# Decode attention with a gated FFN: K in whole 64 KB rows through a ring of three regions, turned in 8 KB pieces

## The chip, the cores and the metric

The kernel runs on one core of one Trainium2 chip. The metric is the device time of one execution in microseconds. Kernels are compared by the median of several runs.

## The reference

One decode step (one query per sequence, two sequences) of 32-head attention over a cache of 4096 keys is mixed by a gate with a small feed-forward network:

```python
# x [2,1,512]; k_cache, v_cache [2,32,4096,128]; wq [512,4096]; wo [4096,512]; w1 [512,1376]; w2 [1376,512]
g = sigmoid((x * gate_w).sum(-1, keepdims=True))
q = (x @ wq) split into 32 heads of 128
scores = einsum("bhqd,bhkd->bhqk", q, k_cache) * 128 ** -0.5
a = (softmax(scores) applied to v_cache, heads joined) @ wo
b = relu(x @ w1) @ w2
out = g * a + (1 - g) * b
```

All inputs are bf16. K and V hold 64 MB each, wq and wo 4 MB each, w1 and w2 1.4 MB each. Each K and V element is used once.

## The kernel before

**Units.** K and V are read as eight units of 8 MB each. A unit is 32768 rows of 128 values; partition p takes 256 of them in a row, so one unit is 64 KB per partition. Units 0 to 3 belong to the first sequence, 4 to 7 to the second; a unit holds eight heads.

**Order by hand.** Every engine has its own list of instructions, written out by the helpers `sp`, `pe`, `dve`, `act` and `pool`. Waits are named markers (`kt_5` is signalled by turn 5), which become semaphore counts. SP issues all large loads, in the order of its list: wq, w1, K, V, wo, w2, and at the end the store. A load whose wait is not met holds up all that follow in that list.

**K.** `kv` has four slots of 32 KB per partition. K comes in sixteen halves of 4 MB (L239), half n into slot n % 4; a half waits until the second turn of the half four back is done. The fourth slot first holds wq, so half 3 waits for the q projection (`pe_qr1`). VectorE transposes each half in two turns of 128x4096 fp32 elements (two bf16 each, L350, `k_turn`) into one of NKT = 3 buffers of 16 KB in `kt`. For each turn TensorE does 16 matmuls of 512 columns (`k_scores`, L372, and L195 in `held`, which keeps the loaded weights): four weight blocks of q, each used for four PSUM banks. A turn waits for the scores of three turns back. All scores add up in four banks, one row for each piece of keys, so that softmax begins only when the last turn's scores are done.

**q.** `qbuf` holds eight blocks. The first sequence's q is written by four ACT instructions (L315) for all units, the second's by `q_second` (L323) after each of units 0 to 3.

**Softmax.** The maximum over the scores (L378), small steps on VectorE, exponentials on ACT (L393), and transposes back (L397). `spread(u)` writes unit u's probabilities into `ptm` on GpSimd, VectorE and ACT (L407, L409, L411).

**V.** Units 0 to 6 are loaded whole (L242) into two regions of 64 KB, each region two slots of `kv`; unit 7 comes in two halves (L245). V's units 0 and 1 wait for the K turns that free their region, unit u >= 2 waits for `pe_v_{u-2}`, the end of the matmuls of the unit two back (64 matmuls, L423).

**End.** wo goes into slot 0 of `kv` after `pe_v_6` (L247, L248), w2 into `kt` (L249, L251). The projection (L469), the FFN (L479), the sum (L487), a copy (L521) and the store (L252) follow.

Of the kernel before, what the change touches and what calls it, by code (L numbers as in the profile page):

```python
# [85 lines left out]
def bass_gated_mix__gqa_block_cached__dense_activation_relu__decode_kernel(  # L86
# [25 lines left out]
    ez1 = sb("ez1", [128, 2], dt.float32)  # L112
    gb = sb("gb", [128, 2], dt.float32)
    gm = sb("gm", [128, 2], dt.float32)
    kv = sb("kv", [128, 4, 16384], dt.bfloat16)
    kt = sb("kt", [128, NKT, 4096], dt.float32)
    qrow = sb("qrow", [128, 2, 4, 128], dt.bfloat16)
    qbuf = sb("qbuf", [128, 8, 4, 160], dt.bfloat16)
    ptm = sb("ptm", [128, 2, 256, 4, 2], dt.bfloat16)
    mpad = sb("mpad", [128, 32], dt.float32)  # L120
    mrow = sb("mrow", [128, 32], dt.float32)
# [15 lines left out]


    flat = kt[:, :, :].rearrange("p k n -> p (k n)")
    kt16 = flat.bitcast(dt.bfloat16).rearrange("p (k r n two) -> p k r n two", k=NKT, r=128, two=2)  # L140
    w1 = flat[:, 0:2752].bitcast(dt.bfloat16)
    E = flat[:, 0:2048].bitcast(dt.bfloat16)
    ET = flat[:, 2048:4096].bitcast(dt.bfloat16)
    w2 = flat[:, 4096:4096 + 2816].bitcast(dt.bfloat16).rearrange("p (r n) -> p r n", n=512)
    X2 = flat[:, 7168:7168 + 1024].rearrange("p (u d) -> p u d", d=128)
    Y = flat[:, 8192:8192 + 512]
    YW = flat[:, 8704:8704 + 512]

    PSF = nc.alloc_psum_tensor("PS", [128, 4096], dt.float32)
    PSB = PSF[:, :].bitcast(dt.bfloat16)  # L150
# [1 line left out]
    def psf(p0, p1, c0, n):  # L152
        return PSF[p0:p1, c0:c0 + n]
# [17 lines left out]
        P.sems[e] = nc.alloc_semaphore(e + "_ev")  # L171
    names = ["x", "gw", "wq", "w1", "wo0", "wo1", "w2a", "w2b", "w2c", "w2d", "out"]
    sem = {n: nc.alloc_semaphore("sem_" + n) for n in names}
    sem_k = [nc.alloc_semaphore(f"sem_k{s}") for s in range(4)]
    sem_v = [nc.alloc_semaphore(f"sem_v{s}") for s in range(3)]

    mk = {}
# [48 lines left out]
    def unit_in(rows, u):  # L226
        return rows[u * 32768:(u + 1) * 32768, :].rearrange("(p r) d -> p (r d)", p=128)

    region = kv[:, :, :].rearrange("p (g s) n -> p g (s n)", g=2)
    wq_sb = kv[:, 3, :].rearrange("p (t u h e d) -> p t u h e d", t=4, u=4, h=4, e=2)  # L230
    wo_sb = kv[:, 0, :]

    act(lambda e: e.dma_start(x_sb[0:2, :], A_x.rearrange("b s d -> (b s) d")).then_inc(sem["x"], 16))
    act(lambda e: e.dma_start(x_sb[2:3, :], gate_w.rearrange("(o d) -> o d", o=1)).then_inc(sem["gw"], 16))
    sp(lambda e: e.dma_start(kv[:, 3, :], wq_in).then_inc(sem["wq"], 16))
    sp(lambda e: e.dma_start(w1, w1_in).then_inc(sem["w1"], 16))
    for n in range(16):
        u, hf = divmod(n, 2)
        sp(lambda e, n=n, u=u, hf=hf: e.dma_start(kv[:, n % 4, :], unit_in(k_rows, u)[:, 16384 * hf:16384 * (hf + 1)]).then_inc(sem_k[n % 4], 16),  # L239
           waits=([f"kt_{2 * (n - 4) + 1}"] if n >= 4 else ["pe_qr1"] if n == 3 else []))  # L240
    for u in range(7):
        sp(lambda e, u=u: e.dma_start(region[:, u % 2, :], unit_in(v_rows, u)).then_inc(sem_v[u % 2], 16),  # L242
           waits=([f"pe_v_{u - 2}"] if u >= 2 else ["kt_27"] if u == 0 else ["kt_31"]))
    for hf in range(2):
        sp(lambda e, hf=hf: e.dma_start(kv[:, 2 + hf, :], unit_in(v_rows, 7)[:, 16384 * hf:16384 * (hf + 1)]).then_inc(sem_v[1 + hf], 16),  # L245
           waits=(["pe_v_5"] if hf == 0 else []))
    sp(lambda e: e.dma_start(wo_sb[:, 0:12288], wo_in[:, 0:12288]).then_inc(sem["wo0"], 16), waits=["pe_v_6"])  # L247
    sp(lambda e: e.dma_start(wo_sb[:, 12288:16384], wo_in[:, 12288:16384]).then_inc(sem["wo1"], 16))  # L248
    sp(lambda e: e.dma_start(w2[0:96, 10, :], B_w2[1280:1376, :]).then_inc(sem["w2a"], 16))  # L249
    for name, r0, r1 in (("w2b", 0, 5), ("w2c", 5, 9), ("w2d", 9, 10)):  # L250
        sp(lambda e, name=name, r0=r0, r1=r1: e.dma_start(w2[:, r0:r1, :], w2_in[:, r0:r1, :]).then_inc(sem[name], 16))  # L251
    sp(lambda e: e.dma_start(out.rearrange("b s (c n) -> (b s c) n", n=256), out_sb[0:128:32, :]).then_inc(sem["out"], 16),  # L252
# [35 lines left out]
    def q_proj():  # L288
        for n in range(8):
            for t in range(4):  # L290
                pe(lambda e, n=n, t=t: e.matmul(  # L291
                    psf(32 * (n % 4), 32 * (n % 4) + 32, (QR_B + n // 4) * BANK, 512), lhsT=xTw[:, t, :],
                    rhs=wq_sb[:, t, n // 2, :, n % 2, :], start=(t == 0), stop=(t == 3), tile_position=(0, 32 * (n % 4))),
                   dwaits=([(sem["wq"], 16)] if n == 0 and t == 0 else []),
                   waits=(["dve_xTw"] if n == 0 and t == 0 else []),
                   signal=(f"pe_qr{n // 4}" if n % 4 == 3 and t == 3 else None))
        for half in range(2):
            row = psf(0, 128, (QR_B + half) * BANK, 512).rearrange("p (h e d two) -> p e h d two", h=4, e=2, two=2)
            for e2 in range(2):
                dst = qrow[:, half, 2 * e2:2 * e2 + 2, :].rearrange("p two (h d) -> p h d two", h=4)  # L300
                src = row[:, e2]
                if half:
                    act(lambda a, dst=dst, src=src: a.activation(out=dst, in_=src, func=ACT.Copy),
                        waits=[f"pe_qr{half}"], signal=f"qrow{half}{e2}")
                else:
                    dve(lambda v, dst=dst, src=src: v.tensor_copy(out=dst, in_=src), waits=[f"pe_qr{half}"], signal=f"qrow{half}{e2}")
        for half in range(2):
            for j in range(4):
                pe(lambda e, half=half, j=j: e.transpose(qT_ps[:, (4 * half + j) * 128:(4 * half + j + 1) * 128],
                                                         qrow[:, half, j, :], ident16[:, :]),  # L310
                   waits=([f"qrow{half}{e2}" for e2 in range(2)] if j == 0 else []),
                   signal=("pe_q" if half and j == 3 else None))
        cols = qT_ps.rearrange("p (f j s m) -> p f s j m", f=2, j=4, s=4)
        for hq in range(4):
            act(lambda a, hq=hq: a.activation(  # L315
                out=qbuf[32 * hq:32 * hq + 32, :, :, 32 + 32 * hq].rearrange("p (f s) j -> p f s j", f=2),
                in_=cols[32 * hq:32 * hq + 32, :, :, :, 0], func=ACT.Copy),
                waits=["pe_q", "c_qbuf"], signal=f"q_0_{hq}")

    def q_second(u):  # L320
        cols = qT_ps.rearrange("p (f j s m) -> p f s j m", f=2, j=4, s=4)
        for hq in range(4):
            act(lambda a, hq=hq: a.activation(  # L323
                out=qbuf[32 * hq:32 * hq + 32, 2 * u:2 * u + 2, :, 32 + 32 * hq],
                in_=cols[32 * hq:32 * hq + 32, u // 2, 2 * (u % 2):2 * (u % 2) + 2, :, 1], func=ACT.Copy),
                waits=[f"pe_sc_{4 * u + 3}"], signal=f"q_1_{u}_{hq}")

    def ffn_h():
        for ft in range(11):
# [14 lines left out]
                signal=f"dve_h{b}")  # L344

    def k_turn(i):
        n, h = divmod(i, 2)
        pairs = kv[:, n % 4, :].bitcast(dt.float32).rearrange("p (r h d) -> p h r d", h=2, d=32)
        dst = kt[:, i % NKT, :].rearrange("p (r n) -> p r n", n=32)
        dve(lambda v: v.transpose(out=dst, in_=pairs[:, h]),  # L350
            waits=([f"pe_sc_{i - NKT}"] if i >= NKT else ["pe_h"] if i == 0 else []),
            dwaits=([(sem_k[n % 4], 16 * (n // 4 + 1))] if h == 0 else []), signal=f"kt_{i}")

    def k_scores(i):
        n, h = divmod(i, 2)
        u, hf = divmod(n, 2)
        for two in range(2):
            for e2 in range(2):
                pos = 4 * u + 2 * hf + e2
                w = qbuf[:, 2 * (u % 4) + e2, 2 * h + two, 32 - pos:160 - pos]  # L360
                first, last = i == 0 and two == 0 and e2 == 0, i == 31 and two == 1 and e2 == 1
                for bk in range(4):
                    head = two == 0 and e2 == 0 and bk == 0
                    waits = [f"kt_{i}"] if head else []
                    if head and i % 4 == 0:
                        waits += [f"q_{u // 4}_{u % 4}_{hq}" if u >= 4 else f"q_0_{hq}" for hq in range(4)]

                    def fn(e, bk=bk, w=w, e2=e2, two=two, first=first, last=last):
                        args = (psf(0, 128, bk * BANK, 512), w, kt16[:, i % NKT, 32 * bk:32 * bk + 32, 16 * e2:16 * e2 + 16, two])
                        if bk:  # L370
                            return held(e, *args, first, last)
                        return e.matmul(args[0], lhsT=args[1], rhs=args[2], start=first, stop=last)  # L372
                    pe(fn, waits=waits, signal=(f"pe_sc_{i}" if two == 1 and e2 == 1 and bk == 3 else None))
        if i % 4 == 3 and u < 4:
            q_second(u)

    def softmax():
        dve(lambda v: v.tensor_reduce(out=mpad[:, 0:1], in_=psf(0, 128, 0, 2048), axis=AX.X, op=ALU.max),  # L378
            waits=["pe_sc_31", "c_mpad"], signal="dve_m")
        dve(lambda v: v.transpose(out=mrow[:, :], in_=mpad[:, :]), waits=["dve_m"], signal="dve_mt")  # L380
        dve(lambda v: v.tensor_reduce(out=mmax[:], in_=mrow[:, :].rearrange("p (u f e) -> p u e f", f=2, e=2), axis=AX.X, op=ALU.max),
            waits=["dve_mt"], signal="dve_mm")
# [108 lines left out]
    gate()  # L491
    selectors()
    q_proj()
    ffn_h()
    for i in range(32):
        k_turn(i)
        if i >= 1:
            k_scores(i - 1)
    k_scores(31)
    softmax()  # L500
    denominators()
    spread(0)
# [51 lines left out]
```

## Time and profile before

| | us |
|---|---|
| median of 3 runs | 345.94 (345.84 to 347.35) |
| the profiled execution | 346.09 |
| its span, first to last instruction | 344.6 |
| busy: TensorE / VectorE / ScalarE / GpSimd | 190.7 / 176.1 / 18.8 / 21.6 |
| moved by DMA | 145.57 MB, mean 422 GB/s |

The span is one profiled execution. PE is TensorE, PEld its weight loads, DVE VectorE, ACT ScalarE, POOL GpSimd, SP the engine that issues the loads. A line "start us, us, engine, line, operation, tiles xcount [idle before <- releaser]" is a row of the timeline. A row of the stretches gives the window, its length, busy time (and instructions) of PE, PEld, DVE, ACT and POOL, the granted TensorE clock, the DMA share and GB/s. The chain of waits is the chain of work that ended last, followed back from the last instruction.

### The profile page before, as it was taken

How to read it: one execution, taken by the hardware profiler on the slowest of the kernel's cores; microseconds unless marked ns; L12 is line 12 of the kernel's file. 1: busy time of each engine (PE TensorE's matmuls, PEld its weight loads, DVE VectorE, ACT ScalarE, POOL GpSimd, SP SyncE). 2: the span in 40 equal slices, each digit the busy share in tenths (PEclk: the TensorE clock that was granted, in tenths of full speed). 3: DMA queues.
4: the chain of work that ended last, by engine and by line, in shares of the span. 5: the costliest groups of instructions: out<-in, count | busy, mean ns of one | idle time of the engine just before them, and what ended most of it. 6: DMA issues, size and time to landing. Idle time of an engine off the chain costs nothing.

```text
span 344.6 us, 2345 instructions
## 1 busy us (share of the span) xinstructions
PE 190.7 (55%) x1226; PEld 40.6 (12%) x842; DVE 176.1 (51%) x93; ACT 18.8 (5%) x48; POOL 21.6 (6%) x33
## 2 busy tenths in 40 slices
PE   0432988877787779877785053215070603215456
PEld 0230100000000000000000021002030201102122
DVE  0708988888998888888985730202010020201021
ACT  1030000000000000000000700000000000000000
POOL 8300000000000000000000230101010010100000
PEclk9965899999999999999999586858567675856566
DMA  8999999999999999999998999999998999999995
GB/s 320 453 424 426 426 426 434 434 415 437 453 436 426 434 426 426 426 426 432 469 464 388 479 398 449 403 457 443 403 479 388 464 413 434 418 411 443 417 415 186
DMA packets 4743, 145.57 MB, mean 422 GB/s; under 512 B 535, under 2 KB 766, under 8 KB 1022
## 3 DMA queue, kind: packets, MB, share of 16 engines
q1 hardware_dynamic: 4728, 145.43, 98.3%
q8 instruction: 8, 0.13, 0.2%
q10 hardware_dynamic: 6, 0.00, 0.0%
q14 instruction: 1, 0.01, 0.0%
HBM read 145.43 MB, written 0.00 MB: 422 GB/s over the span
## 4 chain that ended last, share of the span: by engine, by line
DMA 76%; DVE 12%; PE 9%; ACT 1%; issue 1%; POOL 0%; SPq 0%; DVEq 0%
DMA kv<-in_A_k_cache_dram 38%; DMA kv<-in_A_v_cache_dram 27%; DVE kt L350 10%; DMA kt<-in_B_w_dram 7%; PE PS L423 6%; DMA kv<-in_A_wq_dram 4%; ACT kt L393 1%; PE PS L291 1%; PE PS L195 1%; DVE mpad L378 1%; PE PS L479 1%; POOL ptm L407 0%; DVE kt L397 0%; PE PS L372 0%; PE PS L487 0%
## 5 line engine op out<-in xcount | busy, mean ns | idle before, releaser
L350 DVE STREAM_TRANSPOSE kt<-kv 128x4096 f32<-128x4096 f32 x32 | 140.3, 4424 | 18.9 <-DMA kv<-in_A_k_cache_dram 18.9
L195 PE MATMUL PS<-kt,qbuf 128*128 128x512 bf16 x384 | 113.0, 403 | 0.0
L423 PE MATMUL PS<-kv,ptm 128*32 128x512 bf16 x512 | 45.8, 534 | 86.0 <-DMA kv<-in_A_v_cache_dram 84.9
L372 PE MATMUL PS<-kt,qbuf 128*128 128x512 bf16 x128 | 52.0, 406 | 35.8 <-DVE kt L350 35.8
L429 DVE TENSOR_TENSOR kt<-PS,maskc 128x512 f32<-128x512 f32 x8 | 5.5, 692 | 117.3 <-PE PS L423 117.3
L423 PEld LDWEIGHTS PS<-kv,ptm 128*32 128x32 bf16 x512 | 18.5, 128 | 112.2 <-issue 100.4
L372 PEld LDWEIGHTS PS<-kt,qbuf 128*128 128x128 bf16 x128 | 12.5, 98 | 150.2 <-issue 77.6
L407 POOL COPY ptm<-kt 32x512 bf16<-32x512 bf16 x16 | 11.1, 696 | 273.8 <-DVE rsum L437 184.6
L411 ACT ACTIVATE ptm<-kt 32x512 bf16<-32x512 bf16 x8 | 5.1, 652 | 95.8 <-PE PS L423 94.5
L393 ACT ACTIVATE kt<-PS,negm 128x512 bf16<-128x512 f32 x8 | 5.4, 696 | 80.2 <-DVE negm L389 80.2
L433 DVE TENSOR_REDUCE kt<-kt 128x128 f32<-128x512 f32 x8 | 8.2, 1028 | 0.3
L323 ACT ACTIVATE qbuf<-PS 32x8 bf16<-32x8 bf16 x16 | 3.1, 196 | 85.1 <-PE PS L195 84.8
L440 PE MATMUL PS<-rsum,sell 128*32 128x1 f32 x4 | 0.4, 197 | 10.1 <-DVE rsum L437 10.1
L397 DVE STREAM_TRANSPOSE kt<-kt 128x1024 bf16<-128x1024 bf16 x4 | 5.0, 1245 | 1.7 <-ACT kt L393 1.4
L258 PE MATMUL PS<-ident,x_sb 3*128 3x3 bf16 x4 | 0.3, 168 | 8.1 <-DMA x_sb<-in_gate_w_dram 8.1
L261 DVE COPY xT<-PS 128x12 bf16<-128x12 bf16 x1 | 0.2, 169 | 8.4 <-PE PS L258 8.4
L205 POOL MEMSET qbuf<- 128x5120 bf16 x1 | 4.4, 4358 | 0.0
L378 DVE TENSOR_REDUCE mpad<-PS 128x1 f32<-128x2048 f32 x1 | 2.3, 2291 | 4.0 <-PE PS L195 4.0
L469 PE MATMUL PS<-kv,oW 128*2 128x512 bf16 x32 | 3.7, 621 | 1.1 <-DMA kv<-in_A_wo_dram 1.1
L291 PE MATMUL PS<-kv,xTw 128*32 128x512 bf16 x32 | 3.6, 631 | 0.5 <-DMA kv<-in_A_wq_dram 0.5
L217 POOL MEMSET ptm<- 128x4096 bf16 x1 | 3.5, 3501 | 0.0
L409 DVE COPY ptm<-kt 32x512 bf16<-32x512 bf16 x8 | 3.1, 383 | 0.2
(62 smaller groups left out, 45.2 us busy)
## 6 DMA issues: line engine op xcount, KB each, us to landing
kv<-in_A_k_cache_dram SPq DMA_DIRECT2D x16, 4096.0 KB, 30.0
kv<-in_A_v_cache_dram SPq DMA_DIRECT2D x2, 4096.0 KB, 28.0
kv<-in_A_wq_dram SPq DMA_DIRECT2D x1, 4096.0 KB, 12.2
kv<-in_A_wo_dram SPq DMA_DIRECT2D x1, 3072.0 KB, 20.4
kt<-in_B_w_dram SPq DMA_DIRECT2D x1, 1376.0 KB, 15.0
kv<-in_A_wo_dram SPq DMA_DIRECT2D x1, 1024.0 KB, 22.8
kt<-in_B_w_dram SPq DMA_DIRECT2D x1, 640.0 KB, 23.7
kt<-in_B_w_dram SPq DMA_DIRECT2D x1, 512.0 KB, 24.5
```

Of the source, the lines that this page charges most:

```text
L195: return e.add_instruction(mybir.InstMatmult(start_tensor_calc=start, stop_tensor_calc=stop, tile_size=(128, 128), tile_position=(0, 0), l ...
L291: pe(lambda e, n=n, t=t: e.matmul(psf(32 * (n % 4), 32 * (n % 4) + 32, (QR_B + n // 4) * BANK, 512), lhsT=xTw[:, t, :], rhs=wq_sb[:, t, n ...
L350: dve(lambda v: v.transpose(out=dst, in_=pairs[:, h]), waits=([f"pe_sc_{i - NKT}"] if i >= NKT else ["pe_h"] if i == 0 else []), dwaits=([ ...
L372: return e.matmul(args[0], lhsT=args[1], rhs=args[2], start=first, stop=last)
L378: dve(lambda v: v.tensor_reduce(out=mpad[:, 0:1], in_=psf(0, 128, 0, 2048), axis=AX.X, op=ALU.max), waits=["pe_sc_31", "c_mpad"], signal=" ...
L393: act(lambda a, bk=bk, e2=e2: a.activation(out=blocks[:, bk, :, 16 * e2:16 * e2 + 16], in_=psf(0, 128, bk * BANK, 512).rearrange("p (r n) ...
L397: dve(lambda v, bk=bk: v.transpose(out=ET[:, 1024 * bk:1024 * bk + 1024], in_=E[:, 1024 * bk:1024 * bk + 1024]), waits=[f"act_exp{bk}{e2}" ...
L407: pool(lambda e, args=args: e.tensor_copy(**args), waits=waits, signal=f"pt_{u}_{hq}")
L411: act(lambda e, args=args: e.activation(func=ACT.Copy, **args), waits=waits, signal=f"pt_{u}_{hq}")
L423: pe(lambda e, m=m, t=t: e.matmul(psf(32 * t, 32 * t + 32, V_B[u % 2] * BANK, 512), lhsT=ptm[:, u % 2, 4 * m:4 * m + 4, :, :], rhs=rows[:, ...
L429: dve(lambda e: e.tensor_tensor(out=Y.rearrange("p (c d) -> p c d", c=4), in0=psf(0, 128, V_B[u % 2] * BANK, 512).rearrange("p (c d) -> p ...
L433: dve(lambda e: e.tensor_reduce(out=X2[:, u, :], in_=Y.rearrange("p (c d) -> p d c", c=4), axis=AX.X, op=ALU.add), waits=[f"dve_y{u}"], si ...
```

## The change

- `kv` gets a fifth slot of 32 KB. K moves in ten segments instead of sixteen halves: units 1 to 6 whole, 8 MB each, into the two 64 KB regions in turn; units 0 and 7 in halves of 4 MB, into the fifth slot. The order is u0 first half, u1, u2, u0 second half, u3, u4, u7 first half, u5, u6, u7 second half. A segment waits for the last turn of the segment three back; segment 2 for the q projection.
- The buffers of `kt` shrink from 16 to 8 KB per partition. A turn transposes 128x2048 elements, so there are 64 of them, each with 8 matmuls on two of the four banks (the other `rr`, the other two banks).
- `qbuf` holds two segments' blocks instead of all eight. `q_put(g)` writes the block of segment g (four ACT instructions) after the scores of segment g - 2.
- wo is loaded into the fifth slot and waits for the last turn (`kt_63`); w2 moves to the start of `kt` and waits for the spread of unit 7. Their place in SP's list, behind V's unit 7, is as before. `ET`, `X2`, `Y` and `YW` move within `kt` and `qbuf`.

```diff
-    kv = sb("kv", [128, 4, 16384], dt.bfloat16)
-    kt = sb("kt", [128, NKT, 4096], dt.float32)
+    kv = sb("kv", [128, 5, 16384], dt.bfloat16)
+    kt = sb("kt", [128, NKT, 2048], dt.float32)
...
-    qbuf = sb("qbuf", [128, 8, 4, 160], dt.bfloat16)
+    qbuf = sb("qbuf", [128, 2, 2, 4, 160], dt.bfloat16)
...
-    wo_sb = kv[:, 0, :]
+    wo_sb = kv[:, 4, :]
+    segments = [(0, (0,)), (1, (0, 1)), (2, (0, 1)), (0, (1,)), (3, (0, 1)), (4, (0, 1)), (7, (0,)), (5, (0, 1)), (6, (0, 1)), (7, (1,))]
+    pieces = []
+    for g, (u, halves) in enumerate(segments):
+        for hf in halves:
+            for h in range(2):
+                for rr in range(2):
+                    pieces.append((g, u, hf, h, rr))
...
+    def place(g):
+        return (4, 0, 2)[g % 3]
...
-    for n in range(16):
-        u, hf = divmod(n, 2)
-        sp(lambda e, n=n, u=u, hf=hf: e.dma_start(kv[:, n % 4, :], unit_in(k_rows, u)[:, 16384 * hf:16384 * (hf + 1)]).then_inc(sem_k[n % 4], 16),
-           waits=([f"kt_{2 * (n - 4) + 1}"] if n >= 4 else ["pe_qr1"] if n == 3 else []))
+    for g, (u, halves) in enumerate(segments):
+        dst = kv[:, 4, :] if len(halves) == 1 else region[:, place(g) // 2, :]
+        src = unit_in(k_rows, u)[:, 16384 * halves[0]:16384 * (halves[-1] + 1)]
+        sp(lambda e, g=g, dst=dst, src=src: e.dma_start(dst, src).then_inc(sem_k[g % 3], 16),
+           waits=([f"kt_{last_of[g - 3]}"] if g >= 3 else ["pe_qr1"] if g == 2 else []))
     for u in range(7):
         sp(lambda e, u=u: e.dma_start(region[:, u % 2, :], unit_in(v_rows, u)).then_inc(sem_v[u % 2], 16),
-           waits=([f"pe_v_{u - 2}"] if u >= 2 else ["kt_27"] if u == 0 else ["kt_31"]))
+           waits=([f"pe_v_{u - 2}"] if u >= 2 else [f"kt_{last_of[7]}"] if u == 0 else [f"kt_{last_of[8]}"]))
...
-    sp(lambda e: e.dma_start(wo_sb[:, 0:12288], wo_in[:, 0:12288]).then_inc(sem["wo0"], 16), waits=["pe_v_6"])
+    sp(lambda e: e.dma_start(wo_sb[:, 0:12288], wo_in[:, 0:12288]).then_inc(sem["wo0"], 16), waits=["kt_63"])
...
-    sp(lambda e: e.dma_start(w2[0:96, 10, :], B_w2[1280:1376, :]).then_inc(sem["w2a"], 16))
+    sp(lambda e: e.dma_start(w2[0:96, 10, :], B_w2[1280:1376, :]).then_inc(sem["w2a"], 16),
+       waits=[f"pt_7_{hq}" for hq in range(4)])
...
+    def q_put(g):
+        b, u4 = divmod(segments[g][0], 4)
         cols = qT_ps.rearrange("p (f j s m) -> p f s j m", f=2, j=4, s=4)
         for hq in range(4):
             act(lambda a, hq=hq: a.activation(
+                out=qbuf[32 * hq:32 * hq + 32, g % 2, :, :, 32 + 32 * hq],
+                in_=cols[32 * hq:32 * hq + 32, u4 // 2, 2 * (u4 % 2):2 * (u4 % 2) + 2, :, b], func=ACT.Copy),
+                waits=(["pe_q", "c_qbuf"] if g < 2 else [f"pe_sc_{last_of[g - 2]}"]), signal=f"q_{g}_{hq}")
...
     def k_turn(i):
-        n, h = divmod(i, 2)
-        pairs = kv[:, n % 4, :].bitcast(dt.float32).rearrange("p (r h d) -> p h r d", h=2, d=32)
+        g, u, hf, h, rr = pieces[i]
+        slot = place(g) + (hf if len(segments[g][1]) == 2 else 0)
+        pairs = kv[:, slot, :].bitcast(dt.float32).rearrange("p (r h d) -> p h r d", h=2, d=32)
         dst = kt[:, i % NKT, :].rearrange("p (r n) -> p r n", n=32)
-        dve(lambda v: v.transpose(out=dst, in_=pairs[:, h]),
+        dve(lambda v: v.transpose(out=dst, in_=pairs[:, h, 64 * rr:64 * rr + 64]),
             waits=([f"pe_sc_{i - NKT}"] if i >= NKT else ["pe_h"] if i == 0 else []),
-            dwaits=([(sem_k[n % 4], 16 * (n // 4 + 1))] if h == 0 else []), signal=f"kt_{i}")
+            dwaits=([(sem_k[g % 3], 16 * (g // 3 + 1))] if i == first_of[g] else []), signal=f"kt_{i}")
...
-                for bk in range(4):
+                for bk in range(2):
...
-                        args = (psf(0, 128, bk * BANK, 512), w, kt16[:, i % NKT, 32 * bk:32 * bk + 32, 16 * e2:16 * e2 + 16, two])
+                        args = (psf(0, 128, (2 * rr + bk) * BANK, 512), w, kt16[:, i % NKT, 32 * bk:32 * bk + 32, 16 * e2:16 * e2 + 16, two])
```

More of the change, by code (lines that the diff above doesn't have):

```diff
@@ L139, in bass_gated_mix__gqa_block_cached__dense_activation_relu__decode_kernel @@
     flat = kt[:, :, :].rearrange("p k n -> p (k n)")
-    kt16 = flat.bitcast(dt.bfloat16).rearrange("p (k r n two) -> p k r n two", k=NKT, r=128, two=2)
+    kt16 = flat.bitcast(dt.bfloat16).rearrange("p (k r n two) -> p k r n two", k=NKT, r=64, two=2)
     w1 = flat[:, 0:2752].bitcast(dt.bfloat16)
     E = flat[:, 0:2048].bitcast(dt.bfloat16)
[L143 to L147, printed above, removed]
+    ET = flat[:, 4096:6144].bitcast(dt.bfloat16)
+    w2 = flat[:, 0:2816].bitcast(dt.bfloat16).rearrange("p (r n) -> p r n", n=512)
+    X2 = flat[:, 3072:4096].rearrange("p (u d) -> p u d", d=128)
+    qflat = qbuf[:, :, :, :, :].rearrange("p s e j c -> p (s e j c)").bitcast(dt.float32)
+    Y = qflat[:, 0:512]
+    YW = qflat[:, 512:1024]
     PSF = nc.alloc_psum_tensor("PS", [128, 4096], dt.float32)
@@ L173, in bass_gated_mix__gqa_block_cached__dense_activation_relu__decode_kernel @@
     sem = {n: nc.alloc_semaphore("sem_" + n) for n in names}
-    sem_k = [nc.alloc_semaphore(f"sem_k{s}") for s in range(4)]
+    sem_k = [nc.alloc_semaphore(f"sem_k{s}") for s in range(3)]
     sem_v = [nc.alloc_semaphore(f"sem_v{s}") for s in range(3)]
@@ L227, in unit_in @@
         return rows[u * 32768:(u + 1) * 32768, :].rearrange("(p r) d -> p (r d)", p=128)
-    region = kv[:, :, :].rearrange("p (g s) n -> p g (s n)", g=2)
+    region = kv[:, 0:4, :].rearrange("p (g s) n -> p g (s n)", g=2)
     wq_sb = kv[:, 3, :].rearrange("p (t u h e d) -> p t u h e d", t=4, u=4, h=4, e=2)
-    wo_sb = kv[:, 0, :]
+    wo_sb = kv[:, 4, :]
[6 more added lines that the diff above has]
+                    pieces.append((g, u, hf, h, rr))
+    last_of = {p[0]: i for i, p in enumerate(pieces)}
+    first_of = {}
+    for i, p in enumerate(pieces):
+        first_of.setdefault(p[0], i)
+    def place(g):
+        return (4, 0, 2)[g % 3]
     act(lambda e: e.dma_start(x_sb[0:2, :], A_x.rearrange("b s d -> (b s) d")).then_inc(sem["x"], 16))
@@ L315, in q_proj @@
             act(lambda a, hq=hq: a.activation(
[L316 to L326, printed above, removed]
+                out=qbuf[32 * hq:32 * hq + 32, g % 2, :, :, 32 + 32 * hq],
+                in_=cols[32 * hq:32 * hq + 32, u4 // 2, 2 * (u4 % 2):2 * (u4 % 2) + 2, :, b], func=ACT.Copy),
+                waits=(["pe_q", "c_qbuf"] if g < 2 else [f"pe_sc_{last_of[g - 2]}"]), signal=f"q_{g}_{hq}")
     def ffn_h():
@@ L346, in k_turn @@
     def k_turn(i):
-        n, h = divmod(i, 2)
-        pairs = kv[:, n % 4, :].bitcast(dt.float32).rearrange("p (r h d) -> p h r d", h=2, d=32)
+        g, u, hf, h, rr = pieces[i]
+        slot = place(g) + (hf if len(segments[g][1]) == 2 else 0)
+        pairs = kv[:, slot, :].bitcast(dt.float32).rearrange("p (r h d) -> p h r d", h=2, d=32)
         dst = kt[:, i % NKT, :].rearrange("p (r n) -> p r n", n=32)
-        dve(lambda v: v.transpose(out=dst, in_=pairs[:, h]),
+        dve(lambda v: v.transpose(out=dst, in_=pairs[:, h, 64 * rr:64 * rr + 64]),
             waits=([f"pe_sc_{i - NKT}"] if i >= NKT else ["pe_h"] if i == 0 else []),
-            dwaits=([(sem_k[n % 4], 16 * (n // 4 + 1))] if h == 0 else []), signal=f"kt_{i}")
+            dwaits=([(sem_k[g % 3], 16 * (g // 3 + 1))] if i == first_of[g] else []), signal=f"kt_{i}")
     def k_scores(i):
-        n, h = divmod(i, 2)
-        u, hf = divmod(n, 2)
+        g, u, hf, h, rr = pieces[i]
         for two in range(2):
@@ L359, in k_scores @@
                 pos = 4 * u + 2 * hf + e2
-                w = qbuf[:, 2 * (u % 4) + e2, 2 * h + two, 32 - pos:160 - pos]
-                first, last = i == 0 and two == 0 and e2 == 0, i == 31 and two == 1 and e2 == 1
-                for bk in range(4):
+                w = qbuf[:, g % 2, e2, 2 * h + two, 32 - pos:160 - pos]
+                first, last = i < 2 and two == 0 and e2 == 0, i > 61 and two == 1 and e2 == 1
+                for bk in range(2):
                     head = two == 0 and e2 == 0 and bk == 0
                     waits = [f"kt_{i}"] if head else []
-                    if head and i % 4 == 0:
-                        waits += [f"q_{u // 4}_{u % 4}_{hq}" if u >= 4 else f"q_0_{hq}" for hq in range(4)]
+                    if head and i == first_of[g]:
+                        waits += [f"q_{g}_{hq}" for hq in range(4)]
                     def fn(e, bk=bk, w=w, e2=e2, two=two, first=first, last=last):
-                        args = (psf(0, 128, bk * BANK, 512), w, kt16[:, i % NKT, 32 * bk:32 * bk + 32, 16 * e2:16 * e2 + 16, two])
+                        args = (psf(0, 128, (2 * rr + bk) * BANK, 512), w, kt16[:, i % NKT, 32 * bk:32 * bk + 32, 16 * e2:16 * e2 + 16, two])
                         if bk:
@@ L372, in fn @@
                         return e.matmul(args[0], lhsT=args[1], rhs=args[2], start=first, stop=last)
-                    pe(fn, waits=waits, signal=(f"pe_sc_{i}" if two == 1 and e2 == 1 and bk == 3 else None))
-        if i % 4 == 3 and u < 4:
-            q_second(u)
+                    pe(fn, waits=waits, signal=(f"pe_sc_{i}" if two == 1 and e2 == 1 and bk == 1 else None))
+        if i == last_of[g] and g + 2 < len(segments):
+            q_put(g + 2)
     def softmax():
         dve(lambda v: v.tensor_reduce(out=mpad[:, 0:1], in_=psf(0, 128, 0, 2048), axis=AX.X, op=ALU.max),
-            waits=["pe_sc_31", "c_mpad"], signal="dve_m")
+            waits=["pe_sc_63", "c_mpad"], signal="dve_m")
         dve(lambda v: v.transpose(out=mrow[:, :], in_=mpad[:, :]), waits=["dve_m"], signal="dve_mt")
@@ L493, in bass_gated_mix__gqa_block_cached__dense_activation_relu__decode_kernel @@
     q_proj()
+    q_put(0)
+    q_put(1)
     ffn_h()
-    for i in range(32):
+    for i in range(64):
         k_turn(i)
@@ L498, in bass_gated_mix__gqa_block_cached__dense_activation_relu__decode_kernel @@
             k_scores(i - 1)
-    k_scores(31)
+    k_scores(63)
     softmax()
```

## The prediction

> **What bounds the kernel now.** I read the page first (engines, slices), then the chain of waits, SP's own waits, and last the timeline of VectorE and TensorE around the seam between K and V.
>
> ```profile
> span 344.6 us, 2345 instructions
> PE 190.7 (55%) x1226; PEld 40.6 (12%) x842; DVE 176.1 (51%) x93; ACT 18.8 (5%) x48; POOL 21.6 (6%) x33
> DMA  8999999999999999999998999999998999999995
> DMA packets 4743, 145.57 MB, mean 422 GB/s; under 512 B 535, under 2 KB 766, under 8 KB 1022
> ```
>
> No compute engine is busy for more than 55%, while the DMA row stands at 9 in nearly every slice. The chain names DMA for 76% of the span. So the time is bytes over rate, plus whatever gaps the queue has. The stretches by windows give the rate in the two long phases:
>
> ```profile
> 60.00:160.00 100.00, 80.43 (x328) 7.94 (x83) 90.48 (x22) 2.35 (x12) 0.00 (x0) 1.00 1.00 430
> 210.00:300.00 90.00, 28.49 (x332) 12.59 (x332) 11.02 (x17) 3.29 (x5) 6.39 (x10) 0.69 0.99 430
> 315.00:339.00 24.00, 11.62 (x108) 4.22 (x112) 4.01 (x6) 0.00 (x0) 0.00 (x0) 0.62 0.99 413
> ```
>
> The last columns are the granted clock, DMA share and GB/s. K (first row, rows of 32 KB) and V (second, rows of 64 KB) move at the same 430. Bytes do not change, so the edit can only win or lose gaps, and a gap needs SP to issue a load later than the load ahead of it ends. SP's waits are long (L239 122.4 us in 12 times): each load is issued long before its turn. The place to watch is the seam:
>
> ```profile
> 163.62 8.77 DVE L350 STREAM_TRANSPOSE kt<-kv 128x4096 f32<-128x4096 f32 x2 [1.03 <-DMA kv<-in_A_k_cache_dram]
> 173.34 8.77 DVE L350 STREAM_TRANSPOSE kt<-kv 128x4096 f32<-128x4096 f32 x2 [0.94 <-DMA kv<-in_A_k_cache_dram]
> 186.14 2.29 DVE L378 TENSOR_REDUCE mpad<-PS 128x1 f32<-128x2048 f32 x1 [4.03 <-PE PS L195]
> ...
> 197.75 5.38 PE L423 MATMUL PS<-kv,ptm 128*32 128x512 bf16 x64 [1.16 <-POOL ptm L407]
> 212.10 5.04 PE L423 MATMUL PS<-kv,ptm 128*32 128x512 bf16 x64 [8.97 <-DMA kv<-in_A_v_cache_dram]
> 231.45 5.59 PE L423 MATMUL PS<-kv,ptm 128*32 128x512 bf16 x64 [14.32 <-DMA kv<-in_A_v_cache_dram]
> ```
>
> K's last 4 MB land at 173.3 and are turned in 8.8 us; softmax and V's unit 0 follow; its end at 203.17 lets SP issue V's unit 2. V's unit 1 lands at 212.0, so that issue has 8.8 us to spare. Landings are 9.72 us apart for 4 MB of K, and 19.35 for 8 MB of V.
>
> **Part 1, whole rows for K's units 1 to 6.** Two K halves take 19.44 us, one V unit 19.35: 0.09 us less for 8 MB in rows of 64 KB. Six units: 0.5 us gained. The bounds are 0 (the windows show 430 for both) and 0.6.
>
> [...]
>
> **Part 2, pieces of 8 KB.** 32 turns become 64. A 128x4096 transpose takes 4.42 us, two take 8.77 (start to start 4.35); a 128x32 one (L389) takes 0.19. The line through both gives 0.19 + 2016 x 1.042 ns = 2.29 us for 2048 elements, 2.22 start to start with the same overlap of 0.07. Bounds: half of 4.35, 2.18, and 2.33 if nothing overlaps. Per 4 MB that is 8.9 us against 8.77, below the 9.72 in which they arrive.
>
> TensorE does 8 matmuls for each piece with four weight loads (128 more in all). In the old pieces matmuls start every 0.236 us, and the group's first, which carries the weight load, comes no later than the others (four in 0.94). So 1.9 us a piece; 2.3 if each of the four loads (98 ns) showed in full. I take 1.9: VectorE stays the slower of the two, or level. With three buffers a turn waits for the scores of three pieces back, 4.4 us old, and never stalls.
>
> The new ACT writes (40 of 0.2 us, in place of 4 and 16) come a whole segment ahead of their reader: 9 us or more cover them, nothing else runs on ACT there, and uncovered one set costs 0.8. The memset of qbuf is halved on GpSimd, beside the first load. Both at 0.
>
> **Part 3, the ring.** In units of 4 MB the segments land at 1, 3, 5, 6, 8, 10, 11, 13, 15 and 16, the last four at 124.7, 144.1, 163.6 and 173.3 us. Each is turned at 8.9 us per 4 MB from its landing or the end of the one before. A load waits for the segment three back. Segment 4, for example, waits for segment 1: landed 46.9, turned 64.7; the load ahead of it ends at 76.0. Segments 5, 7, 8 and V's units 0 and 1 have the same 11 us; the others more. No gap there.
>
> The price comes at the end. Before, only 4 MB were unturned when K's last byte landed. Now segment 8 (8 MB) lands at 163.6 and segment 9 queues behind it: twelve pieces, 163.62 + 11 x 2.22 + 2.29 = 190.3, against 182.1. The scores after the last turn shrink from 4.02 to 2.14 us (eight matmuls fewer, 1.88). From the maximum to the end of V's unit 0 is as before, 203.17 - 186.14 = 17.03 us. So V's unit 2 is issued at 190.3 + 2.14 + 17.03 = 209.5, 6.3 us later than now. Behind it on SP only later V loads wait, which are due later.
>
> Is that too late? The first load shows 12.20 us from issue to landing for 4 MB, 2.48 more than the steady 9.72. Issued at 209.5, unit 2 lands at 209.5 + 2.48 + 19.35 = 231.3: when it lands now. Cost 0. The trace's landing records are harsher: twelve of sixteen DMA engines end unit 1 at 210.1 to 210.4, four at 211.2 to 212.0. First packets come 1.0 us after issue and take 2.0 us where steady ones take 1.21, so the early twelve lose about 209.5 + 1.0 - 210.2 + 0.8 = 1.1 us. That lead is not free: the 16 KB instruction fetches each throw one engine back by 1 to 1.7 us, and by the end nine have been hit, some after this point. Between 0 and 1.1 I take 0.8, nearer the packet records.
>
> **Part 4, wo and w2.** Their issue moves from 315.0 to about 295.5, behind V's last halves in SP's order (w2 also behind the last spread, some 1.5 us). The order in the queue is unchanged, and at 315.0 the queue still held V's data until 328. Cost and gain 0. Y and YW in qbuf and E's places change no duration.
>
> **Sum.** The profiled execution took 346.09 (span 344.6 and 1.5 around it), 0.15 over the median 345.94. 346.09 - 0.5 + 0.8 = 346.4.
>
> **Rivals.**
> 1. Slower: V's unit 2 comes clearly late. From 210.2 on (packet records) or 209.5 (landings) each us of delay is a us of time. A piece of 2.33 adds 1.3; V's unit 0 at the 6.14 us that unit 6 takes adds 0.8; scores of 2.5 after the last turn add 0.4. Together the issue is at 212.0 and the gap 2.5 to 3.6: 348.1 to 349.2. Against it: the transpose is regular and its price leaves little room. It decides against "no change" from an issue at about 210.5.
> 2. TensorE's clock falls in the gaps between segments. The row 17:56 of the stretches shows 0.78 after a long idle; half speed means 1.69 us for four matmuls (32.03 to 33.72), 3.4 for a piece. New gaps are 10 us after segment 0 and 2 to 3 us later. The two pieces in hand absorb most of it; before segment 8 it would push the issue by up to 1 us: about 347.4. Against it: the clock stays at 1.00 from 56 to 182 us with waits of 1.6. By the Trainium skill ("TensorE: Matmul & The Clock Gate", Part 1) the clock falls after an idle window of about 3.4 us, which only the first gap reaches; a fall there has 11 us of slack.
> 3. Faster: the end improves because wo and w2 are queued early. The stretch 315:339 runs at 413 against 431; were all of that the late issue, 24 x 18/431 = 1.0 us comes back, with 0.3 in the 19 us ahead: 346.09 - 0.5 - 1.3 = 344.3. Against it: the share is 0.99 there; the rows are 1 to 24 KB, and stay so.
> 4. Much faster: each K load carries a fixed cost like the first load's 2.48 us, and six loads fewer save 14.9 us: 331. Against it: the spacings of 9.72 and 19.35 leave no room for it.
>
> **How the numbers follow.** My sum 0.58; rival 1 0.27, rival 2 0.07, rival 3 0.07, rival 4 0.01. About 0.5% (1.7 us) is what a measurement of this kernel tells from no change, so the sum and half of rival 2 count as same, rival 1 and the rest of rival 2 as slower, and rivals 3 and 4 mostly as faster. Range: downwards 346.09 - 0.6 less half of rival 3's gain, 345.0; upwards rival 1's end, 349.2.
>
> **What would show it.** The turns at 2.2 us start to start and the last one ending near 190; the reduce of the maximum near 192.5; SP issuing V's unit 2 near 209.5 and V's unit 2 landing near 231.3 to 232; K at 19.35 per 8 MB; PEclk at 1.00 through K after 60 us. I am wrong if V's unit 2 lands past 233, if VectorE waits for TensorE within a segment, or if the stretch after 315 changes its rate.

## The result, and the profile after

The changed kernel takes 347.85 us (median of 22 runs, 345.88 to 349.21), the kernel before 346.78 us beside it. The ratio is 1.003, 95% interval 1.0017 to 1.0043: slower by 1.07 us in the medians, and within the 0.5% that the prediction calls no change. 346.4 had been forecast against 345.94, 0.5 us more; the measured difference is twice that, and inside the range. Single executions of 386 us and more (one of the 22 of the kernel before here) are left out of every ratio.

The page of the changed kernel has the same shape: DMA carries the chain, no engine is the bound.

```profile
span 346.5 us, 2520 instructions
PE 199.0 (57%) x1226; PEld 54.3 (16%) x970; DVE 175.1 (51%) x125; ACT 22.3 (6%) x68; POOL 19.5 (6%) x33
DMA  8998998999999998998999999899998999989993
```

The timeline at the seam between K and V (start us, us, engine, line, operation, tiles, count, idle before and its releaser) is the one to lay beside that of before:

```profile
143.76 17.66 DVE L365 STREAM_TRANSPOSE kt<-kv 128x2048 f32<-128x2048 f32 x8 [2.74 <-DMA kv<-in_A_k_cache_dram]
163.00 26.43 DVE L365 STREAM_TRANSPOSE kt<-kv 128x2048 f32<-128x2048 f32 x12 [1.58 <-DMA kv<-in_A_k_cache_dram]
191.59 2.29 DVE L392 TENSOR_REDUCE mpad<-PS 128x1 f32<-128x2048 f32 x1 [2.15 <-PE PS L196]
...
203.20 5.80 PE L437 MATMUL PS<-kv,ptm 128*32 128x512 bf16 x64 [1.16 <-POOL ptm L421]
211.45 5.09 PE L437 MATMUL PS<-kv,ptm 128*32 128x512 bf16 x64 [2.46 <-DMA kv<-in_A_v_cache_dram]
232.32 4.90 PE L437 MATMUL PS<-kv,ptm 128*32 128x512 bf16 x64 [15.78 <-DMA kv<-in_A_v_cache_dram]
...
209.05 0.33 SPq L260 DMA_DIRECT2D kv<-in_A_v_cache_dram  x1
```

Twelve pieces in one row: segment 8 lands at 163.0 and VectorE turns without a pause until 189.43, through segment 9. The maximum starts at 191.59 (186.14 before). The last row is SP's: V's unit 2 is issued at 209.05, where it was 203.17. V's unit 1 is ready at 211.45, 0.65 us earlier than before (212.10). Unit 2 is ready at 232.32, 20.87 us later, though 8 MB need 19.35: a gap of 1.52 us in the stream of loads, and unit 2 is now 0.87 us late. From there on the loads are evenly spaced again, and the delay stays to the end. The chain of waits shows the end (start us, us, what):

```profile
299.70 41.45 DMA kt<-in_B_w_dram
341.19 1.23 PE PS L493 x10
342.43 0.85 PE PS L501 x4
343.28 1.07 PE PS L493 x11
344.37 0.42 DVE out_sb L537
```

The part of w2 that the chain names lands at 299.70 + 41.45 = 341.15. In the kernel before it was 316.36 + 23.71 = 340.07:

```profile
316.36 23.71 DMA kt<-in_B_w_dram
340.11 1.24 PE PS L479 x20
...
342.40 0.42 DVE out_sb L521
```

So w2 lands 1.08 us later, close to the difference of the medians. The profiled spans differ by more, 1.9 us, because TensorE took 3.2 us behind that landing in place of 2.3. That is the granted clock of this one execution. The stretches show it (PE, PEld, DVE, ACT, POOL busy, then granted clock, DMA share, GB/s), first the changed kernel, then the kernel before:

```profile
337.30:344.20 6.90, 5.64 (x76) 1.88 (x68) 0.69 (x1) 0.00 (x0) 0.00 (x0) 0.51 0.53 198
```

```profile
341.30:344.60 3.30, 1.05 (x32) 0.45 (x20) 0.42 (x1) 0.00 (x0) 0.00 (x0) 1.00 0.00 1
```

The times of the kernel before suggest that it does this too in half of its runs: 21 of its 22 times lie at 345.75 to 346.43 and at 346.76 to 347.47. The experiments take up both: the gap, and the end.

### The profile page after: what moved, and what is told of

The parts are those of the page before. It is cut to its first block, busy times and chain, and to the rows that moved or that the text cites. A ratio compares the mean times of both kernels' runs of the same rounds, so it can differ in the third digit from the quotient of the medians.

```text
span 346.5 us, 2520 instructions
## 1 busy us (share of the span) xinstructions
PE 199.0 (57%) x1226; PEld 54.3 (16%) x970; DVE 175.1 (51%) x125; ACT 22.3 (6%) x68; POOL 19.5 (6%) x33
## 4 chain that ended last, share of the span: by engine, by line
DMA 76%; PE 12%; DVE 11%; issue 0%; SPq 0%; DVEq 0%
DMA kv<-in_A_k_cache_dram 32%; DMA kv<-in_A_v_cache_dram 29%; DMA kt<-in_B_w_dram 12%; DVE kt L365 10%; PE PS L437 5%; DMA kv<-in_A_wq_dram 4%; PE PS L386 3%; PE PS L196 2%; PE PS L310 1%; PE PS L493 1%; DVE kt L447 0%; PE PS L501 0%; DVE qbuf L443 0%; DVE out_sb L537 0%; DVE ptm L423 0%
## 5 line engine op out<-in xcount | busy, mean ns | idle before, releaser
L365 DVE STREAM_TRANSPOSE kt<-kv 128x2048 f32<-128x2048 f32 x64 | 141.2, 2274 | 25.4 <-DMA kv<-in_A_k_cache_dram 25.4
L386 PE MATMUL PS<-kt,qbuf 128*128 128x512 bf16 x256 | 107.2, 419 | 33.8 <-DVE kt L365 29.4
L196 PE MATMUL PS<-kt,qbuf 128*128 128x512 bf16 x256 | 106.8, 417 | 0.0
L443 DVE TENSOR_TENSOR qbuf<-PS,maskc 128x512 f32<-128x512 f32 x8 | 5.5, 692 | 113.2 <-PE PS L437 113.2
L386 PEld LDWEIGHTS PS<-kt,qbuf 128*128 128x128 bf16 x256 | 25.9, 101 | 142.8 <-issue 72.9
L337 ACT ACTIVATE qbuf<-PS 32x8 bf16<-32x8 bf16 x40 | 7.8, 196 | 137.5 <-PE PS L196 136.2
L447 DVE TENSOR_REDUCE kt<-qbuf 128x128 f32<-128x512 f32 x8 | 8.2, 1029 | 0.3
L325 DVE CAST qrow<-PS 128x256 bf16<-128x256 f32 x2 | 2.4, 1396 | 3.2 <-PE PS L310 3.2
L461 PE MATMUL PS<-kt,selx 128*32 128x128 f32 x16 | 3.1, 328 | 0.6 <-DVE kt L447 0.6
```

What stands on the lines that cost most here:

```text
L196: return e.add_instruction(mybir.InstMatmult(start_tensor_calc=start, stop_tensor_calc=stop, tile_size=(128, 128), tile_position=(0, 0), l ...
L337: act(lambda a, hq=hq: a.activation(out=qbuf[32 * hq:32 * hq + 32, g % 2, :, :, 32 + 32 * hq], in_=cols[32 * hq:32 * hq + 32, u4 // 2, 2 * ...
L365: dve(lambda v: v.transpose(out=dst, in_=pairs[:, h, 64 * rr:64 * rr + 64]), waits=([f"pe_sc_{i - NKT}"] if i >= NKT else ["pe_h"] if i == ...
L443: dve(lambda e: e.tensor_tensor(out=Y.rearrange("p (c d) -> p c d", c=4), in0=psf(0, 128, V_B[u % 2] * BANK, 512).rearrange("p (c d) -> p ...
L447: dve(lambda e: e.tensor_reduce(out=X2[:, u, :], in_=Y.rearrange("p (c d) -> p d c", c=4), axis=AX.X, op=ALU.add), waits=[f"dve_y{u}"], si ...
```

## The experiments

Each timed experiment was run beside the kernel before, and its ratio is to that. The changed kernel was not run again beside them, so a difference to it is read from the ratios. Rivals A and B, named in the expectations, are that the 64 pieces cost the time (A) or the end of the kernel does (B).

**1. V's unit 2 no longer late.** Its first half goes into the fifth slot, which is free once K's last turn is done.

```diff
     for u in range(7):
+        if u == 2:
+            sp(lambda e: e.dma_start(kv[:, 4, :], unit_in(v_rows, 2)[:, 0:16384]).then_inc(sem_v2, 16), waits=["kt_63"])
+            sp(lambda e: e.dma_start(kv[:, 0, :], unit_in(v_rows, 2)[:, 16384:32768]).then_inc(sem_v[0], 16), waits=["pe_v_0"])
+            continue
...
-    sp(lambda e: e.dma_start(wo_sb[:, 0:12288], ...), waits=["kt_63"])
+    sp(lambda e: e.dma_start(wo_sb[:, 0:12288], ...), waits=["pe_v_2"])
```

> The changed kernel with the first half of V's unit 2 loaded into the fifth slot of kv as soon as K's last turn is done (about 189.4 us); the second half waits for V's unit 0 as before. Theory (the 6 us later end of K makes SP issue V's unit 2 when most DMA engines have run dry; a gap of about 1.5 us, less 0.6 won by the 64 KB rows): the queue never runs dry, V's unit 2 lands near 230.7 instead of 232.2, and the time falls by 1.2 to 1.6 us against the changed kernel, to a ratio of about 0.999 to the kernel before. Rival A (64 pieces with 128 more weight loads cost the time): ratio stays at 1.003. Rival B (the end costs it: wo and w2 queued early, or TensorE's clock there): ratio stays at 1.003.

Measured: 346.40 us (12 runs), ratio 0.9997 (0.9985 to 1.001). SP's rows and TensorE's:

```profile
189.48 0.33 SPq L262 DMA_DIRECT2D kv<-in_A_v_cache_dram  x1
209.09 0.33 SPq L263 DMA_DIRECT2D kv<-in_A_v_cache_dram  x1
...
211.48 5.11 PE L446 MATMUL PS<-kv,ptm 128*32 128x512 bf16 x64 [2.44 <-DMA kv<-in_A_v_cache_dram]
221.28 3.60 PE L446 MATMUL PS<-kv,ptm 128*32 128x512 bf16 x32 [4.69 <-DMA kv<-in_A_v_cache_dram]
230.91 3.60 PE L446 MATMUL PS<-kv,ptm 128*32 128x512 bf16 x32 [6.03 <-DMA kv<-in_A_v_cache_dram]
```

K's order, pieces and late end are untouched (unit 1 at 211.48, as in the changed kernel), yet the second half of unit 2 is ready at 230.91, 19.43 us behind unit 1, in place of 20.87. The ratio falls from 1.003 to 0.9997, 1.1 us. (The medians lie 1.45 us apart, but were not taken side by side.) So rivals A and B fall: the gap is the loss.

**2. V's unit 2 later still.**

```diff
-           waits=([f"pe_v_{u - 2}"] if u >= 2 else ...
+           waits=(["pe_v_1"] if u == 2 else [f"pe_v_{u - 2}"] if u >= 2 else ...
```

> The changed kernel with V's unit 2 waiting for the end of V's unit 1 in place of unit 0, so that it is issued near 216.6 instead of 209.1 us. Theory: the queue is already dry at 209.1, so every us of delay is a us of time: 7.5 us more than the changed kernel, about 355.4. Rivals A and B, in which the gap before V's unit 2 is harmless because later loads catch up: 348 to 350.

Measured, one run: 352.37 us. Unit 1 met a full clock and took 3.64 us, so the issue came at 215.06 and not at 216.6:

```profile
215.06 0.80 SPq L260 DMA_DIRECT2D kv<-in_A_v_cache_dram  x2
...
237.16 5.26 PE L437 MATMUL PS<-kv,ptm 128*32 128x512 bf16 x64 [22.13 <-DMA kv<-in_A_v_cache_dram]
```

For 6.0 us of delay unit 2 is ready 4.8 us later, since the last DMA engines, 1.9 us behind the first before the gap, catch up in it; by the last landing (348.44 against 342.72 in the landing records) 5.7 of the 6.0 are paid. The time itself is only 4.5 us over the changed kernel's median, because this execution ended at full clock, 2.6 us behind its last landing where the profile of the changed kernel took 3.8. So 355.4 was wrong by the assumed issue (1.5 us) and by the end. In the stream of loads a us of delay does cost about a us, and nothing later makes it good; the 348 to 350 of rivals A and B are missed too.

**3. Whole units loaded as halves again**, ring and pieces as changed.

```diff
-        sp(lambda e, g=g, dst=dst, src=src: e.dma_start(dst, src).then_inc(sem_k[g % 3], 16),
+        for j, hf in enumerate(halves):
+            src = unit_in(k_rows, u)[:, 16384 * hf:16384 * (hf + 1)]
+            sp(lambda e, g=g, j=j, src=src: e.dma_start(kv[:, place(g) + j, :], src).then_inc((sem_kb if j else sem_k)[g % 3], 16),
```

> The changed kernel with each whole K unit loaded as two halves of 4 MB, each with its own semaphore, so that its turns can begin when the first half has landed; ring, pieces, q blocks, wo and w2 as changed. Theory: the last turn ends near 182 us again, V's unit 2 is issued near 201 to 202, no gap, and the 0.6 us of the long rows are lost: ratio 1.000, within 0.001. Rivals A and B: 1.003 to 1.005, since the pieces and the moved loads are still there and the row gain is not.

Measured: 346.00 us (11 runs), ratio 0.9993 (0.998 to 1.0005).

```profile
163.36 8.89 DVE L366 STREAM_TRANSPOSE kt<-kv 128x2048 f32<-128x2048 f32 x4 [0.82 <-DMA kv<-in_A_k_cache_dram]
173.07 8.89 DVE L366 STREAM_TRANSPOSE kt<-kv 128x2048 f32<-128x2048 f32 x4 [0.82 <-DMA kv<-in_A_k_cache_dram]
184.12 2.29 DVE L394 TENSOR_REDUCE mpad<-PS 128x1 f32<-128x2048 f32 x1 [2.15 <-PE PS L197]
...
201.64 0.33 SPq L261 DMA_DIRECT2D kv<-in_A_v_cache_dram  x1
```

The last turn ends at 181.96 (173.07 + 8.89), unit 2 is issued at 201.64, and the loss is gone with the wo and w2 moves, the pieces and the ring still in. So the lag comes from a whole unit having to land before its first turn.

**4. The pieces alone**, in the kernel before.

```diff
-        dve(lambda v: v.transpose(out=dst, in_=pairs[:, h]),
+        dve(lambda v: v.transpose(out=dst, in_=pairs[:, h, 64 * rr:64 * rr + 64]),
...
-                for bk in range(4):
+                for bk in range(2):
```

> The kernel before with the pieces alone: turns of 128x2048 into three buffers of 8 KB, eight matmuls each; K's sixteen halves, ring of four slots, q and wo as before. Theory: last turn near 182 us, maximum 1.9 us earlier, no gap anywhere: ratio 1.000. Rival A: 1.002 to 1.004, and TensorE falls behind VectorE within a half.

Measured: 346.96 us (12 runs), ratio 1.0009 (0.9996 to 1.0023). The profile's turns take 8.89 us for 4 MB and the maximum starts at 184.13, 2.0 us earlier; the span is 344.3. The median alone would mislead: five runs lie near 345.8 and seven near 347.0, the two levels of the kernel before. No row of its waits has VectorE's turns waiting for TensorE. Rival A has little left, at most the 0.2% that the interval allows.

**5 to 7. The end.** Twelve 512-column matmuls into an unused PSUM bank fill TensorE's idle stretches behind V's last half; in the changed kernel (5), in that of experiment 1 (6), and in the kernel before (7).

```diff
+    def keep(n):
+        for _ in range(n):
+            pe(lambda e: e.matmul(psf(0, 128, 6 * BANK, 512), lhsT=ident16[:, :], rhs=kv[:, 1, 0:512], start=True, stop=True))
...
-    o_gather(1, [0, 1, 2, 3])
+    o_gather(1, [0, 1, 2])
+    keep(2)
+    o_gather(1, [3])
+    keep(3)
     project()      # keep(4) ahead of r == 24
     ffn_f(10, first=True)
+    keep(3)
```

> The changed kernel with twelve extra 512-column matmuls into an unused PSUM bank, placed in TensorE's idle stretches after V's last half (two before the last gather of O, three ahead of the projection, four ahead of its last eight matmuls, three ahead of the w2 matmuls). Theory of the end: whether TensorE's clock is at full or half speed when the last rows of w2 land sets 2.6 to 2.9 or 3.6 to 3.8 us from that landing to the end of the span, and kept busy it stays at full: the span ends 2.6 to 2.9 us after the landing in the profile, and the median falls by 0.5 to 1 us to about 347.0. The gap before V's unit 2 is still there, so the ratio to the kernel before stays above 1.000. Rival (the end is late because wo and w2 are queued early, or the clock has nothing to do with it): no change, or up to 1.5 us more where the extra matmuls delay the projection.

> Both repairs: V's unit 2 with its first half in the fifth slot, and the twelve extra matmuls at the end. Theory: no gap and a fast end in nearly every run: 345.2 to 345.5, ratio 0.996 to 0.998. Rival: 346.4, ratio 1.000, as with V's unit 2 alone.

> The kernel before with the same twelve extra matmuls at the end. Theory of the end: the runs near 347.0 disappear and those near 345.9 stay, median 345.8 to 346.0. If so, the difference to the kernel with both repairs is what the 64 KB rows bring, 0.4 to 0.6 us. Rival: runs still at both levels.

Measured (12 runs each): 347.14 us, ratio 1.0029 (1.0011 to 1.0046); 345.45 us, ratio 0.9977 (0.9965 to 0.9989); 345.88 us, ratio 0.9986 (0.9976 to 0.9997). The kernel before shows the effect purest: eleven of its twelve runs lie within 345.77 and 346.01, and the upper level is gone. Its stretch at the end, to set beside the half clock of the changed kernel above:

```profile
337.00:344.20 7.20, 4.33 (x71) 1.62 (x67) 1.12 (x2) 0.00 (x0) 0.00 (x0) 1.00 0.46 169
```

From the last landing of w2 to the end of the span take 2.6 to 2.9 us where the clock stands at 1.00 there (before, 2, 4, 5, 6, 7, 10) and 3.6 to 3.8 where it is at half (changed kernel, 1, 3, 8). So about 1 us of the kernel's scatter is the clock at its end, in either kernel. For the times of the changed kernel a gain of the repair is not shown: its median is 0.7 lower than in the result above, but its ratio is where it was, and the runs still spread over 346.28 to 349.38. The rest of the scatter has other sources. In two runs (348.03 and 349.38) 1.9 and 2.8 us lie outside the span, where 1.3 to 1.5 is usual; that the moment of the gap is another source is likely and not shown.

Experiment 6 beats both kernels. It has no gap (19.32 us from unit 1 to the second half of unit 2), a full clock at the end in its profile, and all but one of twelve runs between 345.13 and 345.61:

```profile
211.75 3.64 PE L446 MATMUL PS<-kv,ptm 128*32 128x512 bf16 x64 [2.84 <-DMA kv<-in_A_v_cache_dram]
...
231.07 3.55 PE L446 MATMUL PS<-kv,ptm 128*32 128x512 bf16 x32 [6.38 <-DMA kv<-in_A_v_cache_dram]
```

Against experiment 7, taken beside it, it is 0.43 us faster: 0.3 in the spans (medians 344.0 and 344.3), the rest outside them. The long rows are the likely source of the 0.3, but the two kernels differ in the pieces and the ring as well, so it is not isolated.

**8. wo waits for V's unit 6 again**, and w2 behind it.

```diff
-    sp(lambda e: e.dma_start(wo_sb[:, 0:12288], ...), waits=["kt_63"])
+    sp(lambda e: e.dma_start(wo_sb[:, 0:12288], ...), waits=["pe_v_6"])
```

> The changed kernel with wo waiting for the end of V's unit 6 again (and w2 behind it in SP's list), so that both are issued near 316 as before. Theory: nothing changes, the queue holds V's data until 329: 347.5 to 348.2, ratio 1.002 to 1.005. Rival B (the early issue costs the time): the ratio falls to 1.000.

Measured: 348.13 us (6 runs), ratio 1.005 (1.0033 to 1.0068). The ratio does not fall, so the early issue costs nothing. Nor is a gain of it shown: the higher ratio rests on six runs, its interval overlaps that of the changed kernel, and the one profile ends at half clock; its last landing is at 343.09 with a gap of 1.9 us before unit 2 (211.58 to 232.81), where the changed kernel had 1.5.

**9 and 10. An earlier issue without touching a load.** 45 extra matmuls on q's rows, into the unused bank, keep TensorE busy through the softmax; 10 has the twelve at the end as well.

```diff
+    fill(40)
     denominators()
+    fill(5)
     spread(0)
```

> The changed kernel with 45 extra 512-column matmuls into an unused PSUM bank between K's last scores and V's unit 0 (40 ahead of the sums of the denominators, 5 behind), so that TensorE's clock is at full speed when V's unit 0 begins. Nothing of K's order or of the loads is touched. Theory (the moment at which V's unit 2 is issued sets the gap): V's unit 0 takes 3.6 us in place of 5.2 to 6.1, the issue moves from 209.1 to about 207, the first packets come before the early DMA engines are dry at 209.4, V's unit 2 lands near 230.8 to 231.2, and the time falls by about 1.2 us against the changed kernel: ratio 0.998 to 1.0005, the end of the span still at two levels. Rival C (the twelve pieces after segment 8's landing cost by something else than the issue of V's unit 2, for instance DMA contending with VectorE there): ratio stays at 1.003.

> The same with the twelve extra matmuls at the end as well. Theory: no gap and a fast end, 345.4 to 345.9, ratio 0.997 to 0.999, with little spread. Rival C: 347.1 as with the end alone.

Measured (12 runs each): 346.47 us, ratio 0.9999 (0.9983 to 1.0014), and 346.34 us, ratio 0.9992 (0.9972 to 1.0012). Only experiment 10 has a profile to lay beside the others:

```profile
203.21 3.64 PE L437 MATMUL PS<-kv,ptm 128*32 128x512 bf16 x64
211.53 5.19 PE L437 MATMUL PS<-kv,ptm 128*32 128x512 bf16 x64 [4.69 <-DMA kv<-in_A_v_cache_dram]
231.25 5.56 PE L437 MATMUL PS<-kv,ptm 128*32 128x512 bf16 x64 [14.53 <-DMA kv<-in_A_v_cache_dram]
```

V's unit 0 takes 3.64 us in place of 5.80, ends at 206.85, and unit 2 is ready 19.72 us behind unit 1. 2.2 us of earlier issue take 1.15 of the 1.52 us away, and for the first DMA engine to land the gap is nearly gone (209.47 to 228.99 in the landing records, 19.52 us). Rival C falls: the interval of experiment 9 lies below that of the changed kernel. Not as expected: experiment 10 scatters over 345.25 to 349.25, though its profile ends at full clock. In that profile one DMA engine falls behind all others within V's unit 6 (the last landings of units 5 and 6 are 289.16 and 310.05, 20.9 us apart, while the first engines keep 19.35). Followed from packet to packet, it is the engine whose next packet came behind the 16 KB instruction fetch at 293.57 and took 2.92 us. That this explains the runs near 347 is argued, not shown.

## Why the prediction was right, point by point

**Bound.** DMA set the time before and after; the edit won and lost only gaps, as argued.

**Long rows: 0.5 us.** Unit 1 of V is ready 0.65 earlier in the two profiles. Over all profiles, the seven with K in whole units have it at 211.26 to 211.75, the four with K in loads of 4 MB at 211.81 to 212.10: 0.5 apart on average. Against experiment 3, which differs in K's loads alone (their rows and their number), K's last landing is 0.36 earlier (172.62 and 172.98 in the landing records). The term stands, at 0.4 to 0.5.

**Pieces: 2.22 us, no stall.** Twelve take 26.43 with the last at 2.27, so 2.20 start to start. No row shows VectorE waiting for TensorE in the changed kernel. The scores after the last turn took 2.15 (2.14 forecast).

**Moment of the issue: 209.5.** 209.05. The last turn ended at 189.43, not 190.3: 0.6 of it because segment 8 landed 0.6 earlier, as unit 1 did, the rest from pieces of 2.20. That the issue still hit to 0.45 us is in part luck: V's unit 0 took 5.80 us in place of 5.38, which gave 0.4 of the 0.9 back.

**The gap: 0 to 1.1, taken as 0.8.** This is the term that was mis-sized: 1.52. The bound from the first load's 2.48 us (gap 0) was wrong; the packet records were the right view. There the twelve early engines end unit 1 at 209.45 to 210.58; for most, the first packet of unit 2 follows from 210.0 on and takes 3.0 to 3.4 us where steady ones of 64 KB take 2.42. I had moved neither the landing of unit 1 nor the issue for the gain of the rows, and the two did not shift alike (0.65 and 0.45); and the slow first packets cost up to 1.0, not 0.8. (In the kernel before I counted twelve early engines and four late ones; its landing records show eleven and five.)

The rest of that step fits. The four late engines (211.07 to 211.32) have no gap, and fifteen of the sixteen land unit 2 at 230.35 to 231.21. One alone comes at 232.19, and the last one counts. Followed from packet to packet, it is the engine whose next packet came behind the instruction fetch at 218.25 and took 2.91 us. Without that hit the last landing would have been 231.21, 0.54 us behind the 230.67 of a stream without a gap. So the 1.52 is the lost lead of the early engines and the next fetch together: before, such a hit on an engine that was ahead stayed unseen. The prediction names this ("that lead is not free"), but its sum has no term for a hit right behind the gap.

**Sum.** -0.5 + 0.8 = +0.3 over the profiled execution was forecast; -0.65 + 1.52 = +0.87 came at unit 2's landing and +1.08 at w2's, and the medians say +1.07. That the last two agree is in part luck. The two profiled executions differ by 1.74 us, since the clock at the end adds 0.9 and the time outside the span is 0.2 shorter (1.3 in place of 1.5, which no step had). The 0.2 us between unit 2 and w2 stay open. The lower end of the range, 345.0, is 0.2 too high for half of rival 3's 1.3; nothing hangs on it.

**Rivals.** 1 (unit 2 clearly late) had the right mechanism at its lower edge: the issue came at 209.05, before its threshold of 210.5, and the gap of 1.52 stayed below the 2.1 that its packet formula gives there (210.5 + 1.0 - 210.2 + 0.8). 2 (the clock in K's gaps) came true, against the sign "PEclk at 1.00 through K", and cost nothing: see the last section. 3 and 4 did not happen; experiment 8 bears on 3, and six loads fewer gave under 0.7 us where 4 has 14.9. What no step had was the level of the clock at the end, which moves single runs of both kernels by 1 us.

## What to carry to other kernels

When DMA is the bound, look for the one load whose wait ends close to the time its predecessor finishes, and compute that margin in the packet records: here the first DMA engines to run dry counted, not the last landing, and the restart cost slow first packets as well. Larger loads that must land whole before work begins leave more work behind the last landing (here the last turn ended 7.3 us later, at 189.43 in place of 182.11), and this is paid where a buffer is handed to the next phase, unless a free slot bridges it. Where runs lie at two levels, compare the levels and not only the medians.

## What the runs showed of the hardware that was not expected

TensorE's clock fell in gaps that were shorter than 3.4 us. Four stretches of 3.4 us of the changed kernel, two pairs:

```profile
95.00:98.40 3.40, 0.79 (x4) 0.27 (x3) 3.16 (x2) 0.55 (x3) 0.00 (x0) 1.00 1.34 578
98.40:101.80 3.40, 3.40 (x10) 0.59 (x5) 3.40 (x2) 0.00 (x0) 0.00 (x0) 0.50 0.71 308
163.30:166.70 3.40, 1.56 (x7) 0.39 (x4) 3.40 (x2) 0.78 (x4) 0.00 (x0) 0.99 0.92 395
166.70:170.10 3.40, 3.40 (x10) 0.55 (x4) 3.40 (x3) 0.00 (x0) 0.00 (x0) 0.50 0.97 417
```

TensorE was busy for 0.79 and even 1.56 of 3.40 us in the first row of each pair, and the next 3.4 us ran at half clock. The prediction had relied on the Trainium skill's rule ("TensorE: Matmul & The Clock Gate", Part 1) that the clock falls after an idle window of about 3.4 us; here a window less than half busy was enough. The clock records change only at steps of 3.41 us. In the eleven profiles read here, each such step at full clock in which TensorE was busy for less than 0.40 of the time was followed by half clock (the step in which a trace ends aside), and none in which it was busy for more than 0.51; between the two both happened. The fall cost nothing here: the twelve pieces with the fall at 166.7 took 26.43 us, as did the twelve from 114.58 without one, and no wait of VectorE's turns for TensorE is in the trace. With three buffers TensorE may lag by two pieces before VectorE has to wait.

DMA engines that ran dry for half a us (209.45 to 210.0) lost more than the pause: their first 64 KB packets of V's unit 2 took up to 3.4 us (2.42 in the steady stream).

A 16 KB instruction fetch of about 1 us held one engine back by 1.4 us (packet ends at 218.25 and 222.08, 3.83 us apart in place of 2.42). It shows in the time of a load only when the engine becomes the last to land.
